# A long-convolution block with a dense block behind it: PSUM handed out by banks instead of bank pairs

## The chip, the cores and the metric

One core of one Trainium2 chip. The metric is the device time of one execution in microseconds; the time of a kernel is the median of its runs. Times inside a run come from one profiled execution of the same program.

## What is computed

The input is `A_q` (2048 positions of 640 channels), called x. The first block is a long convolution: `k` goes through a short causal filter of four taps per channel, is multiplied by `v`, then convolved along the whole sequence with a filter `ssm_k` per channel, and gates the normalized x. The second block is a dense layer with Mish and a dense layer back. Both add to their input.

```python
kv = k_shift * v                                   # k_shift: 4 taps per channel
y  = irfft(rfft(pad(kv)) * rfft(pad(ssm_k)))[:S] + kv * ssm_D
h  = x + layernorm(x) * y                          # S=2048, D=640
a  = layernorm(h) @ w1 + b1                        # F=1728
h2 = h + (a * tanh(softplus(a))) @ w2
```

## The kernel before, in words

The Fourier transforms are matmuls in two steps. Channels are five blocks of 128 (`NDC`), grouped in three chunks: blocks 0 and 1, blocks 2 and 3, block 4. The names that the steps use, in the order of the data:

- `k1` (L526 to L539): a block of `ssm_k` (`rn`, loaded by `d_n`, L439) is transposed on TensorE in 16 pieces and copied to `kk_s`; `dadd` (L541) adds `ssm_D` to the filter's first tap.
- `kt`, `kts`, `ks`, `kv` (L482 to L521): `k` is transposed, shifted by one on GpSimd, filtered by matmuls with the band matrices `wsh` (made from `coef` on GpSimd), and multiplied by `v` on VectorE out of PSUM.
- `s1k`, `s1v` (L446 to L470): the first step of the transform, for the filter and for kv, 16 matmuls of 64 rows a unit, 20 units each. `s2k` (22 units, L566) and `s2v` (20 units, L602) are the second step, with the table G (`d_g`).
- `sw`: DMAs that swap real and imaginary rows of the filter's transform; `p1`, `p2` (L617, L621): the product of the transforms on VectorE.
- `i1` (20 units, L653 and L654) and `i2` (one unit a position tile, three parts a, b, c, L713): the inverse. `y` copies an i2 unit out of PSUM.
- `ln1` (statistics of x on VectorE), `ln1p` (GpSimd), `lnx` (normalized x); `wb` and `h` (gate and sum), `bn` (statistics of h), `pow` (GpSimd), `hc` (normalized h), then a transpose to `lnhT` by TensorE (`trpe`, `trev`, first four tiles) or by DMA (`trd`, L750).
- `m1` (L789) and `hb` (Mish on ScalarE, L797): the dense layer in, by five units of 256, 256, 512, 512, 512 positions, 14 feature blocks each; `m2` (L807), `res` (addition, L814) and `d_out` (L816): the dense layer back, by 16 tiles of 128 positions.

Each of these is an operation with a name, an engine, what it depends on and the PSUM space that it takes. The order of the work is a list written out by hand, `ORDER` (L26): every word is an operation and its engine (t TensorE, a ScalarE, v VectorE, p GpSimd, d SyncE's DMA queue, s ScalarE's DMA queue). `_schedule` (L140) walks the list with a cost for each operation, gives each its planned start and its PSUM slot, and the operations are emitted in the order of planned starts. The engines then run their own instructions in that order and wait for each other by semaphores.

PSUM is four tiles, `ps0` to `ps3`, of two banks each (128 partitions by 1024 float32). A unit (`_RT(R_PS)`) takes one whole tile, TensorE fills both banks, and one instruction on ScalarE or VectorE empties both (`ev`, L365 to L369). The next unit that gets the tile waits for that. Even a small unit takes a whole tile.

The first DMAs stand in SyncE's queue: the constants `cst` (identity, the transform's cosines and sines, masks), then the filter blocks 1, 2, 0, 4, and so on; the shift taps and `ssm_D` stand in ScalarE's. Ten matmuls on zeros (`wm`, L389) run while the first loads are under way. The table for Mish is loaded by the instruction `warm` (L380).

Of the kernel before, what the change touches and what calls it, by code (L numbers as in the profile page):

```python
# [16 lines left out]
S = 2048  # L17
# [9 lines left out]
d_id:d d_n1:d cz:v d_n2:d wz:v wm:t cfpe:t coef:v k1pe1:t k1pe2:t k1ev2:v warm:a d_n0:d k1ev1:a k1pe0:t k1ev0:v d_n4:d k1pe4:t k1ev4:v kz:p wsh1:p  # L27
dadd1:p dadd2:p s1kpe2_0:t s1kpe2_1:t s1kpe2_2:t s1kev2_1:v d_a12:d d_k2:d dadd4:p s1kpe2_3:t s1kev2_0:a s1kev2_2:a s1kpe4_2:t d_k0:d s1kpe1_1:t
s1kev2_3:a d_n3:d s1kev4_2:v s1kpe4_0:t s1kpe1_0:t d_k1:d d_x0:d s1kev1_1:a dadd0:p wsh3:p s1kpe4_3:t s1kpe0_3:t s1kev4_0:v s1kev1_0:a d_k3:d
s1kev0_3:a s1kev4_3:v s1kpe4_1:t s1kev4_1:a k1pe3:t k1ev3:v ln1_2:v s1kpe0_1:t s1kpe0_2:t s1kev0_1:a s1kpe1_3:t ktpe1_0:t ktpe0_0:t ln1_1:v s1kev0_2:a  # L30
ktpe1_1:t s1kev1_3:a ktpe0_1:t ktpe1_2:t ktpe0_2:t ktpe2_0:t ktpe1_3:t d_v1:d ktpe0_3:t d_g6:d d_v0:d ktev1:v ktpe2_1:t ktpe3_0:t ktev0:a dadd3:p
ktpe2_2:t ktpe3_1:t ktpe2_3:t ktpe4_0:t ktev2:a ktpe3_2:t ln1_3:v ktsh0:p wsh0:p ktpe4_1:t ktpe3_3:t d_g7:d d_g3:d d_g2:d ktpe4_2:t ktpe4_3:t
s1kpe3_3:t ktev3:v s1kpe1_2:t s1kev3_3:a s1kpe0_0:t s1kpe3_0:t s1kev1_2:a ktev4:v ktsh4:p ktsh1:p s1kev0_0:v ln1_0:v s1kpe3_2:t s1kev3_0:a s1kpe3_1:t
kspe0_1:t s1kev3_1:a ln1p0:p kspe0_0:t s1kev3_2:a kspe4_0:t s2kpe_16:t s2kev_16:a kv0_1:v kv0_0:v kspe4_1:t kv4_0:v s2kpe_9:t s2kev_9:a kv4_1:v
kspe1_0:t s2kpe_6:t s2kev_6:a s2kpe_20:t kspe1_1:t d_g5:d d_g4:d d_g0:d ktsh2:p ln1p3:p wsh2:p kv1_0:v ktsh3:p s2kpe_18:t s2kev_20:a s2kpe_17:t
s2kev_18:a kv1_1:v s2kev_17:a kspe3_1:t s2kpe_8:t s2kev_8:a s2kpe_15:t kv3_1:v s1vpe0_3:t s2kev_15:a s1vpe1_0:t kspe3_0:t s2kpe_21:t s1vev0_3:v
s1vev1_0:a s2kpe_14:t kv3_0:v s2kev_21:a s2kpe_13:t s2kev_14:a s2kpe_19:t s2kpe_0:t s2kpe_11:t s2kev_13:v s2kev_19:a s2kev_0:a s2kpe_10:t s2kev_10:a
d_g1:d s2kpe_4:t s2kpe_12:t s2kev_11:v s2kev_4:v s2kev_12:a s1vpe1_1:t s1vev1_1:v s1vpe0_0:t s1vpe0_2:t s1vev0_2:v s1vpe0_1:t s1vpe1_3:t s1vev0_0:a
s1vev0_1:a s1vev1_3:a s1vpe1_2:t s1vev1_2:v s1vpe3_0:t s2kpe_1:t s1vev3_0:a s2kpe_2:t s2kpe_3:t s2kev_2:a s2kev_1:v kspe2_0:t s2kpe_7:t s2kev_3:v
s2kpe_5:t s2kev_7:a kv2_0:v sw0_1:d kspe2_1:t s2kev_5:a s2vpe0_4:t kv2_1:v s2vpe0_7:t s2vev0_4:a s2vpe0_1:t s2vev0_1:a s2vpe0_2:t s2vev0_2:a  # L40
s2vev0_7:v p2_0_4:v s1vpe4_3:t s2vpe0_3:t s2vev0_3:a s2vpe0_5:t s1vev4_3:v s2vpe0_6:t s2vev0_6:a s1vpe3_2:t s1vev3_2:a s2vev0_5:v p1_0_4:v p2_0_5:v
s1vpe2_1:t p2_0_6:v s1vev2_1:v p2_0_7:v s1vpe2_2:t s1vev2_2:a sw0_0:d s1vpe4_2:t s1vpe3_3:t s1vev4_2:a s1vev3_3:a s1vpe3_1:t s1vpe4_0:t s1vev4_0:v
s1vpe2_3:t p2_0_1:v p2_0_2:v s1vpe2_0:t s1vev3_1:a s1vev2_0:a s1vpe4_1:t s1vev2_3:a s2vpe0_0:t s2vpe1_7:t s2vev0_0:a s2vpe1_5:t s2vev1_7:a s2vev1_5:a
s2vpe1_2:t s2vpe1_0:t s2vev1_0:a s2vpe1_4:t s2vev1_4:a s1vev4_1:a p1_0_5:v p1_0_6:v p1_0_2:v p1_0_1:v sw1_0:d p2_0_0:v s2vev1_2:v p2_1_0:v p2_0_3:v
p1_0_0:v sw1_1:d p1_0_7:v p1_0_3:v p2_1_4:v s2vpe1_3:t s2vpe1_6:t s2vpe1_1:t d_x2:d sw2_1:d s2vev1_6:a s2vpe2_3:t s2vev1_3:a p2_1_3:v s2vev1_1:a
s2vev2_3:a s2vpe2_2:t p2_1_7:v p2_1_6:v p1_1_0:v i1pe0_1:t i1ev0_1:a p2_1_5:v p2_1_1:v s2vpe2_1:t s2vev2_1:a s2vev2_2:a sw2_0:d p2_1_2:v p1_1_4:v
p1_1_2:v p1_1_1:v p1_1_3:v p1_1_6:v p1_1_7:v i1pe0_2:t i1pe0_0:t i1ev0_0:a i1pe0_7:t i1ev0_7:a s2vpe2_0:t i1ev0_2:a i1pe0_4:t i1ev0_4:a s2vev2_0:a
i1pe0_6:t i1ev0_6:a i1pe0_3:t p1_1_5:v i1ev0_3:a i1pe0_5:t i1ev0_5:a i1pe1_2:t i1pe1_0:t i1pe1_6:t i1ev1_0:a i1ev1_6:a i1pe1_1:t i1ev1_1:a i1pe1_7:t
p2_2_2:v p1_2_2:v p2_2_3:v d_w11:d d_w13:d i1ev1_2:a i1ev1_7:a p2_2_1:v p2_2_0:v p1_2_1:v p1_2_0:v i1pe1_4:t i1ev1_4:a p1_2_3:v ln1_15:v ln1_11:v
ln1_12:v i1pe2_2:t i1pe1_3:t i1ev2_2:v i1ev1_3:a i1pe2_0:t i1pe2_1:t i1ev2_1:v i1ev2_0:a i1pe1_5:t ln1_13:v d_w14:d d_t2m:d d_w12:d i1pe2_3:t d_x1:d  # L50
i1ev1_5:a d_w10:d d_w2:d i2pa0:t i2pa1:t i2pb0:t i2pa2:t i2pb1:t i1ev2_3:a i2pc0:t y0:a i2pc1:t d_small:p y1:v b1pe:t i2pb2:t ln1p2:p i2pc2:t w1z:p
ln1p1:p gate:p lnx0:p c_b1:a y2:a lnx1:p i2pa9:t i2pa3:t i2pb9:t i2pc9:t y9:a i2pb3:t i2pa12:t i2pc3:t y3:a i2pb12:t i2pa7:t i2pc12:t y12:a i2pb7:t
i2pa4:t i2pc7:t y7:a lnx3:p ln1p15:p lnx2:p wb1:v wb0:v i2pb4:t i2pa13:t h0:v h1:v bn0:v ln1p13:p pow0:p i2pc4:t y4:a bn1:v i2pb13:t i2pa5:t i2pc13:t
y13:a i2pb5:t i2pa14:t i2pc5:t hc0:v i2pb14:t trpe0:t pow1:p y5:a wb2:v hc1:v i2pc14:t y14:a i2pa10:t trpe1:t i2pb10:t trev0:v i2pa15:t wb3:v i2pa11:t
i2pb15:t i2pb11:t i2pc15:t i2pc10:t trev1:a i2pc11:t m1pe0_6:t y10:a y15:a m1pe0_0:t hb0_0:a y11:a m1pe0_2:t m1pe0_5:t hb0_6:a hb0_2:a hb0_5:a i2pa6:t
m1pe0_4:t ln1_7:v ln1p7:p h3:v ln1p12:p h2:v bn3:v pow3:p bn2:v lnx7:p ln1_4:v pow2:p hc2:v hc3:v i2pb6:t trpe2:t i2pc6:t m1pe0_3:t ln1_6:v lnx12:p
ln1p11:p lnx11:p ln1p6:p hb0_4:a ln1_8:v ln1_9:v ln1_5:v ln1_14:v trpe3:t y6:a trev2:a trev3:a w2z:p ln1p4:p lnx4:p m1pe0_1:t m1pe1_0:t hb0_3:a
m1pe1_1:t hb0_1:a lnx6:a wb4:v hb1_1:a ln1p9:p ln1p8:p ln1p5:p m1pe1_6:t lnx15:a wb6:v i2pa8:t hb1_6:a m1pe1_2:t i2pb8:t m1pe1_4:t i2pc8:t hb1_2:a
h4:v bn4:v pow4:p hb1_0:a lnx13:a lnx5:p ln1_10:v ln1p10:p wb5:v wb15:v wb13:v h13:v hc4:v wb7:v m2pe1:t m1pe1_3:t lnx10:a y8:v h5:v bn5:v hb1_3:a
pow5:p h7:v h6:v bn7:v pow7:p hc5:v bn6:v lnx8:a res1:v wb8:v lnx9:a hb1_4:a trd4:d pow6:p trd5:d wb10:v h10:v hc6:v trd6:d m1pe1_5:t hb1_5:a m2pe0:t  # L60
hc7:v res0:v m2pe2:t m2pe3:t h8:v bn8:v res2:v trd7:d m1pe2_3:t pow8:p wb12:v m1pe2_2:t wb11:v h11:v h15:v hc8:v res3:v bn10:v wb9:v bn15:v h9:v
m1pe2_0:t hb2_0:a hb2_2:a pow10:p d_out3:d m1pe2_6:t hc10:v bn11:v pow11:p bn9:v trd8:d hc11:v ln1p14:p pow9:p hc9:v h12:v m1pe2_4:t m1pe2_1:t hb2_3:a
hb2_6:a m1pe2_5:t lnx14:a hb2_1:a hb2_5:a bn12:v trd11:d pow12:p hb2_4:a bn13:v trd10:d trd9:d m1pe3_2:t pow15:p wb14:v h14:v bn14:v pow14:p hc12:v
trd12:d m1pe3_0:t hc15:v d_out2:d m1pe3_5:t hb3_5:a hb3_2:a hb3_0:a m1pe3_4:t m2pe6:t m1pe3_6:t hc14:v trd15:d trd14:d d_out0:d hb3_4:a hb3_6:a
m1pe3_1:t m1pe3_3:t res6:v pow13:p hb3_1:a hb3_3:a hc13:v m2pe5:t m2pe4:t m2pe7:t trd13:d d_out6:d res5:v res4:v d_out4:d res7:v m2pe11:t m2pe10:t
res11:v res10:v m1pe4_6:t m1pe4_0:t hb4_0:a hb4_6:a m2pe8:t m1pe4_2:t m1pe4_1:t hb4_2:a m1pe4_4:t m1pe4_5:t hb4_4:a m1pe4_3:t hb4_1:a m2pe9:t hb4_3:a
res9:v hb4_5:a res8:v m2pe14:t m2pe15:t res14:v m2pe13:t d_out7:d d_out9:d d_out5:d d_out11:d d_out1:d res13:v res15:v d_out13:d d_out14:d m2pe12:t
res12:v d_out15:d d_out10:d d_out8:d d_out12:d
""".split()
UNITS = [256, 256, 512, 512, 512]  # L70
# [13 lines left out]
class _Ring:  # L84
# [3 lines left out]
    def free(self):  # L88
        best = None
        for i, rt in enumerate(self.held):  # L90
            t = 0.0
            for u in rt.users if rt is not None else ():
                if not u.done:
                    break
                t = max(t, u.finish + u.lat + _TAIL[u.eng] + _HOP)
            else:
                if best is None or t < best[0]:
                    best = (t, i)
        return best


class _RT:


    def __init__(self, ring):
        self.ring = ring
        self.users = []
        self.tile = None


class _Op:
    def __init__(self, name, opts, deps, allocs, uses, emit, prio, lat):
        self.name = name
        self.opts = opts
        self.deps = [d for d in deps if d is not None]
# [24 lines left out]
def _schedule(ops):  # L140
# [6 lines left out]
    for word in ORDER:  # L147
# [24 lines left out]
        for rt in o.allocs:  # L172
            rt.slot = rt.ring.free()[1]
            rt.ring.held[rt.slot] = rt
# [9 lines left out]
def _dve1(n):  # L184
    return 0.06 + 0.001045 * n
# [671 lines left out]
```

## Time and profile before

| | us |
|---|---|
| runs: median (lowest to highest) | 231.36 (230.88 to 232.72) |
| profiled execution, its own time | 229.75 |
| its span, first to last instruction | 227.9 |
| TensorE busy | 217.6 (95%) |
| VectorE busy | 143.4 (63%) |
| ScalarE busy | 132.5 (58%) |
| GpSimd busy | 51.6 (23%) |

How to read it: the span is cut into stretches, and busy time in a stretch says which engine is full there. A share over the whole span is an average over stretches with different limits. Matmuls overlap in the array, so that a TensorE that is busy is not yet at its peak; the distance between the starts of two matmuls is their price. The same holds for casts on ScalarE and VectorE: one lasts longer than the distance to the next. The chain of waits leads back from the last instruction to what released it, step by step.

### The profile page before, as it was taken

The numbers are of one execution on the slowest core, as the hardware profiler recorded it, in microseconds if no ns is written. First come the engines' busy times: TensorE is split into PE (matmuls) and PEld (weight loads), VectorE is DVE, ScalarE is ACT, GpSimd is POOL, SyncE is SP. The second block draws the span as 40 slices with busy tenths as digits, with TensorE's granted clock in tenths as the row PEclk, the third lists the DMA queues.
The fourth block names the chain that finished last, engine by engine and source line by source line (L and its number), as shares of the span: only waits on it lengthen the run. The fifth ranks groups of instructions, "written<-read, shape, count | busy, mean of one in ns | idle before, by whom it ended". The sixth has DMA issues, their size and how long they took to land.

```text
span 227.9 us, 6283 instructions
## 1 busy us (share of the span) xinstructions
PE 217.6 (95%) x2718; PEld 164.6 (72%) x2718; DVE 143.4 (63%) x289; ACT 132.5 (58%) x180; POOL 51.6 (23%) x87
## 2 busy tenths in 40 slices
PE   7989999999879999989999999999999999999993
PEld 2889899999768999878877754445567766447772
DVE  0697998999999999899999998810202120002121
ACT  2388979989999999878966004748240004244000
POOL 0550675000000546149852113210000000000000
PEclk9999999999999999999999999999999999999999
DMA  6999991066898495930001421442200100000304
GB/s 189 417 396 423 415 405 39 4 186 171 250 265 237 109 344 183 384 126 1 3 0 29 83 64 20 69 91 58 58 0 3 58 0 3 0 0 1 117 4 169
DMA packets 27086, 30.60 MB, mean 134 GB/s; under 512 B 9201, under 2 KB 23474, under 8 KB 26674
## 3 DMA queue, kind: packets, MB, share of 16 engines
q1 hardware_dynamic: 26944, 30.19, 40.7%
q8 instruction: 21, 0.34, 0.7%
q14 instruction: 7, 0.06, 0.1%
q10 hardware_dynamic: 50, 0.01, 0.0%
q0 software_dynamic: 64, 0.00, 0.0%
HBM read 20.37 MB, written 2.62 MB: 101 GB/s over the span
## 4 chain that ended last, share of the span: by engine, by line
PE 79%; ACT 9%; DVE 5%; DMA 3%; issue 2%; SPq 1%; POOL 0%; DVEq 0%; ACTq 0%
PE ps L807 27%; PE ps L789 27%; ACT uv L367 7%; PE ps L654 4%; PE ps L653 4%; PE ps L460 4%; DMA rn<-in_A_ssm_k_dram 3%; PE ps L566 2%; PE ps L490 2%; ACT uk L367 2%; PE ps L713 2%; PE ps L513 2%; PE ps L461 2%; DVE uv L369 2%; PE ps L602 2%
## 5 line engine op out<-in xcount | busy, mean ns | idle before, releaser
L797 ACT ACTIVATE uv<-ps,b1s 128x512 bf16<-128x512 f32 (+1 forms) x70 | 36.5, 608 | 59.8 <-PE ps L789 59.8
L789 PE MATMUL ps<-G 128*128 128x512 bf16 (+1 forms) x350 | 62.5, 336 | 0.0
L807 PE MATMUL ps<-rn,uv 128*128 128x320 bf16 x448 | 61.8, 299 | 0.0
L807 PEld LDWEIGHTS <-uv 128*128 128x128 bf16 x448 | 43.8, 98 | 17.5
L789 PEld LDWEIGHTS <-G 128*128 128x128 bf16 x350 | 34.1, 98 | 25.8
L367 ACT CAST uk<-ps 128x1024 bf16<-128x1024 f32 (+2 forms) x50 | 46.6, 1093 | 6.3 <-PE ps L461 3.8
L814 DVE TENSOR_TENSOR xa<-ps,xa 128x640 bf16<-128x640 f32 x6 | 4.9, 823 | 49.0 <-PE ps L807 49.0
L367 ACT CAST uv<-ps 128x1024 bf16<-128x1024 f32 x30 | 28.5, 1095 | 0.0
L653 PE MATMUL ps<-a,uv 128*128 128x128 bf16 x160 | 18.7, 219 | 0.0
L653 PEld LDWEIGHTS <-uv 128*128 128x128 bf16 x160 | 17.8, 113 | 0.1
L738 POOL TENSOR_TENSOR r<-ve,mhalf 128x1 f32<-128x1 f32 x16 | 9.5, 595 | 28.5 <-DVE ve L735 28.4
L814 DVE TENSOR_TENSOR xb<-ps,xb 128x640 bf16<-128x640 f32 x6 | 4.9, 823 | 17.1 <-PE ps L807 14.9
L692 POOL TENSOR_TENSOR r<-ve,mhalf 128x1 f32<-128x1 f32 x16 | 12.7, 797 | 6.9 <-DVE ve L688 6.8
L602 PE MATMUL ps<-uv,G 128*128 128x64 bf16 (+1 forms) x384 | 12.6, 187 | 1.7 <-ACT uv L367 1.7
L369 DVE CAST uk<-ps 128x1024 bf16<-128x1024 f32 (+1 forms) x12 | 13.9, 1191 | 0.4 <-ACT uk L367 0.2
L602 PEld LDWEIGHTS <-G 128*128 128x128 bf16 x384 | 11.7, 96 | 2.4 <-issue 2.2
L617 DVE TENSOR_TENSOR uv<-uv,uk 128x1024 bf16<-128x1024 bf16 x20 | 12.6, 688 | 0.1
L519 DVE TENSOR_TENSOR ra<-ps,rb 128x1024 bf16<-128x1024 f32 x10 | 11.7, 1218 | 1.0 <-PE ps L514 1.0
L369 DVE CAST uv<-ps 128x1024 bf16<-128x1024 f32 x10 | 12.0, 1220 | 0.3 <-PE ps L461 0.2
L460 PE MATMUL ps<-cst,ra 128*64 128x128 bf16 x160 | 10.8, 219 | 1.1 <-ACT uv L367 0.8
L461 PE MATMUL ps<-cst,ra 128*64 128x128 bf16 x160 | 11.0, 221 | 0.0
L713 PE MATMUL ps<-uk,ra 128*128 128x256 bf16 (+1 forms) x96 | 10.7, 255 | 0.2
(103 smaller groups left out, 337.3 us busy)
## 6 DMA issues: line engine op xcount, KB each, us to landing
G<-tab_g SPq DMA_DIRECT2D x8, 512.0 KB, 13.5
rn<-in_A_ssm_k_dram SPq DMA_DIRECT2D x5, 512.0 KB, 5.6
ra<-in_A_k_dram SPq DMA_DIRECT2D x4, 640.0 KB, 7.6
rb<-in_A_v_dram SPq DMA_DIRECT2D x2, 1280.0 KB, 11.0
G<-in_B_w_dram SPq DMA_DIRECT2D x5, 432.0 KB, 6.1
rn<-in_B_w_dram SPq DMA_DIRECT2D x1, 2080.0 KB, 11.5
rn<-uk SPq DMA_DIRECT2D x4, 512.0 KB, 6.5
rb<-uk SPq DMA_DIRECT2D x8, 256.0 KB, 7.7
```

Of the source, the lines that this page charges most:

```text
L367: nc.scalar.copy(o, i)
L369: nc.vector.tensor_copy(o, i)
L460: nc.tensor.matmul(ps[0:64, dgl, :], lhs, mc, start=True, stop=True)
L461: nc.tensor.matmul(ps[64:128, dgl, :], lhs, ms, start=True, stop=True)
L602: nc.tensor.matmul(ps[:, fl * st:fl * st + n], g_v[:, f0 + fl, :], V[c.i][:, :, f0 + fl, :], start=True, stop=True)
L617: nc.vector.tensor_tensor(v, v, K[c.i][:, :, f0:f1, :], ALU.mult)
L653: nc.tensor.matmul(pz[:, dgl, :], V[c.i][:, dg // 4, :, dg % 4], a12[:, 0, :], start=True, stop=False)
L692: nc.gpsimd.tensor_tensor(r1[:, t2:t2 + 1], ve1[:, t2:t2 + 1], mhalf[:, 0:1], ALU.pow)
L713: nc.tensor.matmul(py[:, o:o + w], t2m[:, t2, ri, :], Z[c.i][:, ri * NT + t2, o - c.c0:o - c.c0 + w], start=(ri == 0), stop=(ri == 1))
L789: nc.tensor.matmul(ph[:, i * 512:i * 512 + w], w1[:, dc, fc * P:fc * P + P], lnhT_of(u)[:, dc, 0:w], start=(dc == 0), stop=(dc == NDC - 1))
L797: nc.scalar.activation(hb_of(u)[:, fc, 0:w], rt.tile[:, i * 512:i * 512 + w], ACT.Mish, bias=b1s[:, fc:fc + 1], scale=1.0)
L807: nc.tensor.matmul(po[:, a * 512:a * 512 + 320], hb_of(u)[:, fc, tl * P:(tl + 1) * P], w2[:, fc, a * 320:a * 320 + 320], start=(fc == 0), ...
```

## The change

- PSUM is given out by single banks. The four tiles stay, and a slot is now one half of a tile (eight slots); a unit can still take both halves of a tile. Of two banks that are free equally early the one is taken whose neighbour comes free later.
- The units of `k1`, `ks`/`kv`, `s1k`, `s1v`, `s2k`, `s2v` and `i1` can be done in halves, x and y: half of the matmuls into one bank and an eviction of that bank. The list chooses for each: nearly all `s1`, `s2k`, `ks`, `i1` units are halves, 10 of 20 `s2v` units are whole. `m1` is 70 units of one feature block instead of 35 of two; `m2` and `res` are two halves of 320 columns a tile, 448 and 192 for the last tile, whose output DMA is also in two parts.
- The filter block 1 is loaded and transposed by halves of 64 partitions (`d_n1a`, `d_n1b`), and block 0 is loaded first.
- The identity is a table of its own; identity, the rest of the constants, the shift taps and `ssm_D` are four DMAs in ScalarE's queue. `wm` has seven matmuls instead of ten.
- `ORDER` is a new list throughout. Among other things it has `warm` behind four copies and a cast on ScalarE, the first half of V behind seven blocks of G, the last piece of x behind `w2`, and five `ln1` instead of eight ahead of the last `i1` eviction.

The core of the diff:

```diff
+class _Banks(_Ring):
+    def free(self, est, wide):
+        t = [self.when(i) for i in range(len(self.held))]
+        if wide:
+            i = min(range(0, len(t), 2), key=lambda i: max(t[i], t[i + 1]))
+            at = max(t[i], t[i + 1])
+        else:
+            i = min(range(len(t)), key=lambda i: (max(t[i], est), -t[i ^ 1]))
+            at = t[i]
+        assert at < 1e9
+        return at, i
...
-    R_PS = _Ring(4)
+    R_PS = _Banks(8)
...
     def ps_f32(rt):
-        rt.tile = banks[rt.slot][:]
+        o = rt.slot % 2 * 512
+        rt.tile = banks[rt.slot // 2][:, o:o + (1024 if rt.wide else 512)]
         return rt.tile
...
+        if not whole_only and (_BOTH or ev_name + "x" in names):
+            for h in range(2):
+                rt = _RT(R_PS, False)
+                pes.append(OP(pe_name + "xy"[h], ("pe", dur / 2), deps, allocs=[rt], emit=lambda e, rt=rt, h=h: pe(ps_f32(rt), h)))
+                outs.append(OP(ev_name + "xy"[h], evs(cols // 2), pes[-1:], uses=[rt], emit=lambda e, rt=rt, h=h: evf(e, rt.tile, h)))
...
-        for _ in range(10):
+        for _ in range(7):
             nc.tensor.matmul(ps[:, 0:512], wz[:, 0:P], wz[:, P:D], start=True, stop=True)
...
+    d_id = OP("d_id", ("dmaS", 0.42), emit=lambda e: nc.scalar.dma_start(idn[:], dram["idn"]), lat=1.4)
+    d_cst = OP("d_cst", ("dmaS", 0.42), emit=lambda e: nc.scalar.dma_start(cst[:], dram["cst"]), lat=3.3)
...
+    def emit_kn1(h):
+        return lambda: nc.sync.dma_start(raw_n[1][64 * h:64 * h + 64], A_ssm_k.rearrange("(d m l) s -> m d l s", m=NDC, l=4)[1, 16 * h:16 * h + 16])
...
-        for fp in range(NFC // 2):
-            rt = _RT(R_PS)
+        for fc in range(NFC):
+            rt = _RT(R_PS, False)
...
+            for a, (d0, d1) in enumerate(((0, 448), (448, D)) if t2 == NT - 1 else ((0, 320), (320, D))):
+                rt = _RT(R_PS, False)
...
+                    DMA(f"d_out{t2}{'ab'[a]}", 164e3 * (d1 - d0) / D, (lambda t2=t2, d0=d0, d1=d1: nc.sync.dma_start(oview[:, t2, d0:d1], xt(t2)[:, d0:d1])), deps=outs[-1:])
```

## The prediction

> **What bounds the kernel now.** I read the page's slices first, then busy time by stretch, then the chain, then the timelines of ScalarE and VectorE for prices.
>
> ```profile
> PE   7989999999879999989999999999999999999993
> DVE  0697998999999999899999998810202120002121
> ACT  2388979989999999878966004748240004244000
> ```
>
> Forty slices of 5.7 us. TensorE looks full everywhere; VectorE is full up to slice 23 and ScalarE up to slice 16, then both have room. Stretch by stretch:
>
> ```profile
> 5.90:11.60 5.70, 5.40 (x87) 4.93 (x88) 3.94 (x7) 1.87 (x1) 2.94 (x3) 1.00 1.03 417
> 11.60:30.00 18.40, 17.15 (x423) 16.09 (x418) 15.90 (x27) 16.74 (x17) 7.25 (x9) 1.00 1.02 411
> 30.00:40.00 10.00, 10.00 (x192) 9.60 (x189) 9.31 (x8) 8.50 (x11) 6.86 (x12) 1.00 0.49 192
> 40.00:70.80 30.80, 27.97 (x725) 25.75 (x722) 30.31 (x38) 30.15 (x35) 0.00 (x0) 1.00 0.67 187
> 70.80:91.10 20.30, 20.27 (x388) 19.76 (x386) 19.99 (x45) 20.01 (x22) 9.66 (x10) 1.00 0.65 206
> 91.10:101.10 10.00, 9.19 (x98) 7.64 (x96) 8.84 (x27) 8.24 (x15) 2.04 (x4) 1.00 0.81 292
> 101.10:133.30 32.20, 32.20 (x275) 26.09 (x274) 30.72 (x89) 19.20 (x40) 17.42 (x31) 1.00 0.11 22
> 133.30:224.30 91.00, 90.95 (x546) 53.26 (x544) 23.11 (x54) 26.27 (x43) 4.99 (x9) 1.00 0.16 41
> ```
>
> Columns: PE, PEld, DVE, ACT, POOL busy, PE clock, DMA share, GB/s. From 40 to 91 us VectorE and ScalarE, which empty PSUM, are over 98% busy: the front is bound by evictions. From 101 us on TensorE is never idle:
>
> ```profile
> 101.06 4.42 PE ps L789 x40
> 121.87 11.41 PE ps L807 x84
> 133.28 23.74 PE ps L789 x110
> 205.23 19.03 PE ps L807 x140
> 224.28 0.82 DVE xb L814
> ```
>
> L789 runs at 0.216 us for 512 columns, L807 at 0.136 for 320, back to back. So the end is the moment the first L789 can start (101.06), plus 123.2 us of matmuls, plus the tail. The change can win only ahead of 101 us and in the tail.
>
> ```profile
> 7.13 1.87 ACT L367 COPY xa<-ps 128x2048 bf16<-128x2048 bf16 x1 [3.92 <-PE ps L534]
> 11.65 4.68 ACT L367 CAST uk<-ps 128x1024 bf16<-128x1024 f32 x5 [2.65 <-PE ps L461]
> 52.31 20.26 ACT L367 CAST uv<-ps 128x1024 bf16<-128x1024 f32 x22
> 94.28 4.27 ACT L367 CAST rb<-ps 128x640 bf16<-128x640 f32 x7 [0.35 <-PE ps L713]
> ```
>
> ```profile
> 13.63 3.49 DVE L369 CAST uk<-ps 128x1024 bf16<-128x1024 f32 x3 [0.20 <-ACT uk L367]
> 119.32 0.82 DVE L369 CAST rb<-ps 128x640 bf16<-128x640 f32 x1
> 120.06 0.48 DVE L728 TENSOR_TENSOR xa<-rb,xa 128x640 bf16<-128x640 bf16 x1
> ```
>
> Here is the price of a half. One cast lasts 1.10 us (group mean), so 22 in 20.26 us are (20.26-1.10)/21 = 0.91 apart; at 640 columns (4.27-0.69)/6 = 0.60. The slope is 0.82 ns a column, the fixed part 0.07. VectorE: (3.49-1.22)/2 = 1.135 apart at 1024, 0.74 at 640 (119.32 to 120.06): fixed part 0.08.
>
> **The front, as one account of two engines.** The last i1 eviction ends near 92.2 on ScalarE, and VectorE's share of that stage near 91.1. ScalarE first evicts at 7.13, VectorE at 8.37: together 85.1 + 82.7 = 167.8 us, of which the stretches (without the early coef work, and with ScalarE's last microsecond) give 156.7 busy. Idle: 11.1 us over both. Now the terms, counted in the two lists of operations up to the same point.
>
> Halves: ScalarE gets 127 half evictions for 63.5 whole ones, VectorE 73 (20 of them the kv products, 6 bf16 ones) for 36.5. 63.5 x 0.07 + 36.5 x 0.08 = 7.3 us. Bounds: nothing, and 15.6 with fixed parts of 0.157 (Mish rows: 0.577 apart at 512, 0.367 at 256) and 0.155 (VectorE's durations, 1.22 and 0.82). I take the cast rows, which are the same instruction.
>
> Second table load: ScalarE's list now starts with a copy, whose table is loaded ahead of it, and `warm` comes inside the stream: 1.28 + 0.20 us (its rows at 1.71 and 3.01, idle time before). +1.5.
>
> Layer statistics: five ln1 groups instead of eight ahead of that point, 3 x 1.23 = -3.7. Units moved between the engines (five 1024-column ones to VectorE, some s2k and k1 ones to ScalarE), and coef, whose 1.0 us now falls into the stream: +2.7.
>
> Earlier start. The first filter block is SP's first DMA (0.73 for 1.15) and took 4.7 us to its first matmul, so 5.4; eight transposes of 0.067 and a hop: ScalarE at 6.1, not 7.13. VectorE takes the half block behind it at 7.0, not 8.37. -2.4. The three warming matmuls taken out (0.43 each) only end TensorE's cover at 4.4 instead of 5.8. The constants on ScalarE's queue cost four issues of about 0.5 us before 2.6, covered by the empty wait; identity, second there, lands about 2.3 us after 1.15. In SP's queue the first half of V now stands behind seven table blocks: 12.2 MB at 0.41 MB/us from 2 us on, and a landing, about 33 us. VectorE has 28.9 us of listed work ahead of its use, so 36: covered by 3 us. Later there the last piece of x stands behind w2 (2.16 MB, 5.3 us more, landing near 99); its statistics come after hc1, near 103: covered by 4 us. On POOL's queue the w2 zeroing (0.63) and two ln1p (1.16 each) stand ahead of lnx0, 5.6 us in all after the gate, which is due some 8 us before the last i1 eviction: covered.
>
> Sum: 7.3 + 1.5 - 3.7 + 2.7 - 2.4 = +5.4 us over two engines, 2.7 us for the front, plus half of whatever the idle time changes. That last term decides. Zero idle would give 2.7 - 5.6 = -2.9; break-even needs 5.7 of the 11.1 us to go.
>
> Does handing out single banks remove idle time? The tiles ps0 to ps3 still have two banks each, and the changed program's waits are by tile: 86 of the 222 waits that a matmul has for an eviction are for the eviction of its tile's other bank, and 81 of the 166 waits that evictions have for TensorE are for matmuls into the other bank (before: 33 and 20, all at the two-bank m1 units or behind them). So a half is often released only with its neighbour, as a whole unit was; and where plan and program differ, the in-order queues behind stall too. Against that, the other half of the waits is really finer. At the head the profile's 2.65 us gap on ScalarE shrinks to about 1.1 (copies end near 8, first cast near 9), but VectorE gets a new one of about 2.3: its second piece stands behind s1 matmuls that wait for POOL's dadd (0.45). I take idle as before, 11.1.
>
> **Behind the front.** Up to the first m1 unit, 9.9 us today, the change does 12.6 instead of 14 i2 tiles; VectorE's own list (four half evictions 2.4, one ln1 1.2, wb to hc 5.4, transpose and copy about 1.2) is 10.2, so TensorE idles longer: +0.7 (0 to +1.5). The m1 and m2 matmuls keep count and columns; their waits by tile are covered by ScalarE's 65 and VectorE's 68 idle us of 91 (0 to +1). Tail: the last addition has 192 columns, 0.35 for 0.82, and a third of the bytes: -0.6.
>
> Total 2.7 + 0.7 - 0.6 = +2.8: 229.75 becomes 232.55 in the profiled execution. The runs' median, 231.36, lies 1.6 above that execution, so 234.2.
>
> [...] Row: 0.07 and 0.08 us per extra instruction. [...] Row: one table load 1.28 us. [...]
>
> **The rivals.** A: finer hand-out works. Idle falls to the head's 1.1 us, -5.0: 229.2; with the halves' fixed part at its lower bound, nothing, 3.65 less, 225.5; the middle is 227.4. For it: the other waits are for the own bank, and two engines can take one unit's halves at once. Against: the waits by tile. It decides once idle is under 5.7.
> B: idle is halved, -2.8: 231.4, no change. For it: only half of the waits are by tile.
> C: stalls pile up. 54 evictions ahead of m1 wait for a neighbour's fill, 0.22 to 0.45 us each; at 0.22 that is 12 us more idle, +6: 240.2. Against: in a full queue the neighbour is filled long before.
> D: the fixed part is the larger one of the rows, +4.1: 238.3. For it: Mish at 256. Against: the cast rows.
>
> **Chances.** Forecast, idle about as before, 0.32; C and D together 0.14; B 0.36; A 0.18. One per cent is about what a measurement of this kernel can tell from no change. Faster (under 229.0) is A: 0.18. Within it is B: 0.36. Slower (over 233.7): forecast, C and D, 0.46. The range, 227.4 to 238.6, runs from A's middle to D and leaves out half of A and half of C and D; the forecast's own is 232.6 to 236 (idle 8 to 15).
>
> **What would show it.** Right: 512-column casts 0.49 apart on ScalarE and 0.61 on VectorE; first evictions near 6.1 and 7.0; ScalarE and VectorE together still idle 9 to 13 us up to the last i1 eviction, at 94 to 96; first m1 near 104; a table load inside the first casts. Wrong: the last i1 eviction before 92, or halves under 0.46 apart, or matmuls of m1 and m2 no longer back to back.

## The result, and the profile after

The changed kernel takes 265.66 us (265.23 to 266.19), beside 231.12 (229.76 to 232.72) of the kernel before on the same chip: a ratio of 1.149, interval 1.1415 to 1.1571. The sign is that of the forecast, the size is not: +34.5 us where +2.8 was expected, far outside the range.

The 40 slices of the profile's page, for TensorE, VectorE, ScalarE and TensorE's clock:

```profile
PE   6797888777677898898799999899989898979892
DVE  0187887777799899498869996761640000100422
ACT  1568896886899898777477515450011666110000
PEclk9689999999999999999999999999999999999999
```

Before, VectorE stood at 9 in all slices but one from 40 to 136 us, and ScalarE at 8 or 9 up to 91 us. Now, in the slices from 13 to 73 us, VectorE stands at 7 or 8 and ScalarE mostly at 6 or 8, and the front has become longer. The busy time by stretch says it in numbers (columns as before: stretch, its length, then PE, PEld, DVE, ACT, POOL busy, clock, DMA share, GB/s):

```profile
40.00:70.80 30.80, 23.75 (x471) 21.11 (x468) 22.55 (x39) 23.97 (x46) 0.84 (x2) 1.00 0.37 111
70.80:91.10 20.30, 15.31 (x428) 13.56 (x425) 18.75 (x35) 17.95 (x27) 0.00 (x0) 1.00 0.73 220
...
123.90:260.20 136.30, 126.09 (x821) 79.80 (x827) 57.99 (x167) 46.30 (x82) 24.14 (x44) 1.00 0.12 31
```

From 40 to 71 us all three engines are busy for about 75% of the time: no engine is full there, and what fills the rest is waiting. And the dense layers, 123.2 us back to back before, take 136.35, 10.2 of which TensorE idles. Here are pieces of the chain of waits from their end (start, length, engine; L888 is Mish, L899 m2, L904 its addition):

```profile
233.65 0.69 ACT uv L888
...
247.32 0.51 DVE xb L904
247.87 2.08 PE ps L899 x14
249.96 0.50 DVE xb L904
250.51 7.78 PE ps L899 x56
258.31 0.50 DVE xb L904
258.86 1.33 PE ps L899 x14
260.21 0.49 DVE xa L904
```

Before, the chain ran through matmuls alone here. Now it runs through single Mishes and additions too, and behind each of those shown but the last TensorE had stopped for it.

The whole difference splits into three stages. The last column is the experiment that decides most of it, told below: the changed program on tiles of one bank.

| us | before | after | after, one-bank tiles |
|---|---|---|---|
| first eviction, ScalarE / VectorE | 7.13 / 8.37 | 6.71 / 9.84 | 6.56 / 8.55 |
| busy up to the last i1 eviction, both engines | 156.9 | 170.2 | 165.2 |
| idle up to there, both engines | 11.0 | 43.5 | 8.0 |
| last i1 eviction (mean of the two engines) | 91.7 | 115.1 | 94.1 |
| first m1 | 101.06 | 123.86 | 102.16 |
| from there to the end of the last m2 matmul | 123.2 | 136.35 | 124.07 |
| from there to the end of the span | 3.66 | 4.20 | 3.03 |
| span | 227.9 | 264.4 | 229.3 |

### The profile page after: what moved, and what is told of

Read it like the earlier page. It is cut to its first block, busy times and chain, and to the rows that moved or that the text cites. A ratio compares the mean times of both kernels' runs of the same rounds, so it can differ in the third digit from the quotient of the medians.

```text
span 264.4 us, 6418 instructions
## 1 busy us (share of the span) xinstructions
PE 226.7 (86%) x2724; PEld 168.5 (64%) x2731; DVE 149.5 (57%) x343; ACT 142.5 (54%) x245; POOL 48.2 (18%) x88
## 4 chain that ended last, share of the span: by engine, by line
PE 59%; ACT 18%; DVE 8%; DMA 5%; issue 4%; SPq 3%; POOLq 0%; ACTq 0%; POOL 0%; DVEq 0%
PE ps L899 22%; PE ps L883 21%; ACT uk L421 9%; ACT uv L421 6%; PE ps L809 3%; ACT uv L888 3%; DVE uk L423 2%; DMA rn<-in_A_ssm_k_dram 2%; DVE ra L590 2%; SPq L679 2%; PE ps L749 2%; DMA G<-in_B_w_dram 2%; PE ps L662 2%; PE ps L635 2%; PE ps L750 1%
## 5 line engine op out<-in xcount | busy, mean ns | idle before, releaser
L888 ACT ACTIVATE uv<-ps,b1s 128x512 bf16<-128x512 f32 (+1 forms) x70 | 38.2, 604 | 53.8 <-PE ps L883 45.3
L899 PE MATMUL ps<-rn,uv 128*128 128x320 bf16 (+2 forms) x448 | 63.4, 299 | 4.1 <-DVE xb L904 1.7
L899 PEld LDWEIGHTS <-uv 128*128 128x128 bf16 x448 | 43.6, 98 | 23.2 <-issue 4.5
L421 ACT CAST uk<-ps 128x512 bf16<-128x512 f32 (+2 forms) x95 | 50.1, 593 | 13.4 <-PE ps L750 2.4
L421 ACT CAST uv<-ps 128x512 bf16<-128x512 f32 (+1 forms) x46 | 29.9, 720 | 5.0 <-PE ps L699 1.8
L904 DVE TENSOR_TENSOR xa<-ps,xa 128x320 bf16<-128x320 f32 x12 | 5.6, 485 | 41.8 <-PE ps L899 41.8
L423 DVE CAST uk<-ps 128x512 bf16<-128x512 f32 (+2 forms) x27 | 17.5, 673 | 7.9 <-ACT uk L421 5.8
L904 DVE TENSOR_TENSOR xb<-ps,xb 128x320 bf16<-128x320 f32 (+2 forms) x12 | 5.5, 487 | 25.1 <-PE ps L899 25.1
L834 POOL TENSOR_TENSOR r<-ve,mhalf 128x1 f32<-128x1 f32 x16 | 10.3, 645 | 41.3 <-DVE ve L831 41.3
L423 DVE CAST uv<-ps 128x512 bf16<-128x512 f32 x21 | 14.0, 688 | 4.3 <-PE ps L536 2.5
L662 PE MATMUL ps<-uk,G 128*128 128x160 bf16 x128 | 13.1, 230 | 3.7 <-ACT uk L421 2.0
L535 PE MATMUL ps<-cst,ra 128*64 128x128 bf16 x160 | 11.8, 219 | 4.8 <-ACT uv L421 3.1
L590 DVE TENSOR_TENSOR ra<-ps,rb 128x512 bf16<-128x512 f32 x20 | 13.0, 687 | 5.0 <-ACT uk L421 3.8
L421 ACT CAST rb<-ps 128x640 bf16<-128x640 f32 x16 | 10.5, 695 | 8.6 <-PE ps L809 8.6
L715 DVE TENSOR_TENSOR uv<-uv,uk 128x1024 bf16<-128x1024 bf16 x20 | 13.1, 687 | 0.0
```

The lines of the kernel that those rows point to most:

```text
L421: nc.scalar.copy(o, i)
L423: nc.vector.tensor_copy(o, i)
L535: nc.tensor.matmul(ps[0:64, k, :], lhs, mc, start=True, stop=True)
L590: nc.vector.tensor_tensor(kv_w[:, m, :, 8 * h:8 * h + 8, l0:l0 + n], ps.rearrange("p (l t d) -> p d t l", l=n, t=8), raw_v[:, 8 * h:8 * h ...
L662: nc.tensor.matmul(ps[:, o:o + 160], g_v[:, f, :], KA[:, :, f, :], start=True, stop=True)
L715: nc.vector.tensor_tensor(v, v, K[c.i][:, :, f0:f1, :], ALU.mult)
```

## The experiments

Theory 1: the plan gives banks away one by one, but the tiles of PSUM still have two banks and the program waits by tile, so a bank also waits for what happens in its neighbour. The rivals: the price of the additional instructions (2), the head with its clock, table load and DMA queue (3), the new order itself (4).

**Tiles of one bank.** Order, plan and slots stay.

```diff
-    banks = [psum.tile([P, 1024], F32, name=f"ps{i}") for i in range(4)]
+    banks = [psum.tile([P, 512], F32, name=f"ps{i}") for i in range(8)]
...
+        rt.tile = banks[rt.slot][:]
+        if rt.wide:
+            rt.tile = [rt.tile, banks[rt.slot + 1][:]]
...
-            outs.append(OP(ev_name, evs(cols), pes[-1:], uses=[rt], emit=lambda e, rt=rt: evf(e, rt.tile, None)))
+            outs.append(OP(ev_name, evs(cols), pes[-1:], uses=[rt], emit=lambda e, rt=rt: evf(e, rt.tile[0], None) if whole_only else [evf(e, rt.tile[h], h) for h in range(2)]))
...
```

> The changed kernel with PSUM as eight tiles of one bank instead of four of two; same order, same slots; the 35 or so units that take two banks are emptied by two instructions. Theory 1 (the plan gives out banks, but the program waits by tile, so that every half also waits for its neighbour's matmuls and evictions, in the front and in the dense layers): most of the 34 us go, 226 to 238 us, first m1 at 95 to 105, m1 and m2 back to back again (first m1 to last m2 123 to 125). Theory 2 (the fixed price of the halves): two instructions more for each wide unit, 266 to 269. Theory 3 (the head: half clock, second table load, x0 in front of the table G in SP's queue): within 3 us of 265.7. Theory 4 (the new order itself is worse, whatever the waits): over 250.

Measured: 231.39 us, ratio to before 1.0037 (1.0016 to 1.0058). All of the loss but about 1 us is gone, from all three stages. Order, plan and head are those of the changed kernel, so theory 4 (over 250 us) is out, and theories 2 and 3 cannot be the bulk of the loss: the halves and the head are all still there. By stretch:

```profile
40.00:70.80 30.80, 28.72 (x725) 26.16 (x723) 30.21 (x51) 30.80 (x66) 0.00 (x0) 1.00 0.72 205
70.80:91.10 20.30, 20.11 (x400) 19.53 (x398) 19.53 (x40) 19.84 (x42) 2.56 (x6) 1.00 0.69 239
...
102.10:226.20 124.10, 123.72 (x822) 79.96 (x828) 57.87 (x168) 46.44 (x88) 23.96 (x44) 1.00 0.14 35
```

ScalarE is busy for all 30.80 us of the first stretch, where it had 23.97. Its timeline between 40 and 62 us, first of the changed kernel, then of this one:

```profile
42.00 3.03 ACT L421 CAST uk<-ps 128x480 bf16<-128x480 f32 x6 [0.43 <-DVE ra L590]
46.17 1.49 ACT L421 CAST uk<-ps 128x480 bf16<-128x480 f32 x3 [1.15 <-DVE ra L590]
48.06 1.95 ACT L421 CAST uk<-ps 128x480 bf16<-128x480 f32 x4 [0.41 <-PE ps L662]
50.37 0.56 ACT L421 CAST uk<-ps 128x480 bf16<-128x480 f32 x1 [0.36 <-DVE ra L590]
```

```profile
39.67 8.90 ACT L422 CAST uk<-ps 128x480 bf16<-128x480 f32 x19
48.33 1.23 ACT L422 CAST uv<-ps 128x512 bf16<-128x512 f32 x2
49.28 0.74 ACT L422 CAST uk<-ps 128x480 bf16<-128x480 f32 x1
49.73 13.03 ACT L422 CAST uv<-ps 128x512 bf16<-128x512 f32 x26
```

The releaser in the brackets is the tell. A ScalarE cast of the filter (uk) needs nothing that VectorE's kv product (ra, L590) makes; they meet only in a tile of PSUM. On tiles of one bank these brackets are gone. The changed kernel's list of waits has more of the kind, evictions held by the other engine's evictions:

```profile
DVE uk L423 <- ACT uk L421: 5.8, 5, 3.4
DVE ra L590 <- ACT uk L421: 3.8, 6, 1.1
```

The columns are microseconds in all, times, and the longest. With the smaller lines of its kind in the front that is 22 waits and 15.5 us over the two engines. The kernel before has two (1.7 us), the program on tiles of one bank none.

**The dense layers alone.** The kernel before, its front and order unchanged, with slots of one bank on tiles of two, single banks for m1, m2 and the small units, and the last tile in two parts.

```diff
-    R_PS = _Ring(4)
+    R_PS = _Banks(8)
...
-        for fp in range(NFC // 2):
-            rt = _RT(R_PS)
+        for fc in range(NFC):
+            rt = _RT(R_PS, False)
```

> The kernel before with one part of the change: slots of one bank on tiles of two, one bank for the small units, m1 in 70 units of one bank, m2 and its addition in halves, the last tile in two parts; the front's units and the order stay. Theory 1: the front stays as before (first m1 near 101), but m1 and m2 are no longer back to back: first m1 to last m2 128 to 137 instead of 123.2, and the run 236 to 246. Theories 2, 3, 4 (the cause lies in the front alone): 229 to 232; the tail alone would give 0.6.

Measured: 250.17, ratio 1.0864 (1.0813 to 1.0915). First m1 at 102.1, the stage 142.3 instead of 123.2. Theory 1 holds, and the loss is over its upper end. TensorE's and ScalarE's timeline where the third group of positions starts m1:

```profile
135.56 6.64 PE L813 MATMUL ps<-G 128*128 128x512 bf16 x29
...
142.24 0.69 ACT L818 ACTIVATE uv<-ps,b1s 128x512 bf16<-128x512 f32 x1 [15.06 <-PE ps L813]
142.98 1.24 PE L813 MATMUL ps<-G 128*128 128x512 bf16 x5 [0.78 <-ACT uv L818]
...
144.25 2.42 ACT L818 ACTIVATE uv<-ps,b1s 128x512 bf16<-128x512 f32 x4 [1.33 <-PE ps L813]
144.99 1.24 PE L813 MATMUL ps<-G 128*128 128x512 bf16 x5 [0.78 <-ACT uv L818]
```

Six units of five matmuls fill banks (29 of the 30 matmuls are in the trace). The first Mish in ScalarE's list empties the fifth (its tile's first half), but it starts only when the sixth, in the other half, is done. The next matmuls wait 0.78 us for this Mish; the next Mish waits 1.33 us for these, and the matmuls behind them 0.78 us for it. TensorE and ScalarE take turns, twice here and again at 153, 162 and 172 us.

**The same units, on tiles of one bank.** Every two-bank eviction of the front is then two instructions.

> The kernel before with its own order and whole units, on eight tiles of one bank: every eviction of two banks in two instructions, each bank released by itself; m1 in 70 units, m2 in halves, the last tile in two parts as in the change. Theory 1 (waits by tile): m1 and m2 back to back (first m1 to last m2 123 to 124), where the same units on tiles of two banks took 142; the front has the fixed price of the halves (first m1 at 105.4 with whole release) less what the finer release gives: first m1 at 102 to 105, run 231 to 234.5. If small units as such break the dense layers: 245 or more.

Measured: 232.30, ratio 1.0072 (1.005 to 1.0093); first m1 at 104.40, the stage 123.4. At the same place of the program:

```profile
136.62 9.66 PE L824 MATMUL ps<-G 128*128 128x512 bf16 x44
...
142.22 0.69 ACT L829 ACTIVATE uv<-ps,b1s 128x512 bf16<-128x512 f32 x1 [14.35 <-PE ps L824]
143.30 3.00 ACT L829 ACTIVATE uv<-ps,b1s 128x512 bf16<-128x512 f32 x5 [0.39 <-PE ps L824]
```

The first Mish starts 5.60 us after the first matmul (five units of 1.09), where it took 6.68 (six units), and TensorE does not stop. Small units as such cost the dense layers next to nothing.

**Mish earlier in the program.** On tiles of two banks again, each Mish right behind its own m1 unit in the order in which the program is written down.

```diff
+    for o in [o for o in order if o.name.startswith("hb")]:
+        order.remove(o)
+        order.insert([p.name for p in order].index("m1pe" + o.name[2:]) + 1, o)
```

> The kernel before with single banks in the dense layers on tiles of two (250.2), with one edit: each Mish stands in the program right behind the m1 unit that it empties, instead of where its planned start puts it. Theory 1 (waits by tile): the Mish no longer waits for the matmuls of the next unit in its tile's other bank, but these now wait for the Mish, about 0.9 us for most of the 35 pairs: first m1 to last m2 150 to 165, the run 256 to 272. Rival (the evictions only stand too late in the program, and a bank waits for its own eviction alone): matmuls back to back, 229 to 234.

Measured: 272.51, ratio 1.1818 (1.1783 to 1.1853), the stage 164.9 us; the run is half a microsecond over the upper end. The rival is out by 38 us. The waits of the dense layers:

```profile
PEld L813 <- issue: 37.3, 37, 1.6
PE ps L813 <- ACT uv L818: 26.1, 34, 1.1
```

The second line is 34 waits of the m1 matmuls for a Mish, nearly one for each of the 35 pairs of units, where the late Mish had nine (6.9 us); the first line is the idle time of TensorE's weight loads ahead of m1. This order turns the false wait round and does not take it away.

**The price of halves alone.** The kernel before, its two-bank evictions ahead of m1 as two instructions each, for example:

```diff
-                ev(e, (V, K)[which][c.i][:, b0:b0 + 2, :, :], ps)
+                for h in range(2):
+                    ev(e, (V, K)[which][c.i][:, b0 + h:b0 + h + 1, :, :], rt.tile[:, 512 * h:512 * h + 512].rearrange("p (b g f) -> p b f g", b=1, g=4))
```

> The kernel before with each of its two-bank evictions ahead of m1 (k1, s1, kv, s2k, s2v, i1) as two instructions of one bank each; units, order and tiles stay. This is the fixed price of halves alone. The recorded price, 0.07 us on ScalarE and 0.08 on VectorE for each further instruction, some 8 us over two engines that share the work: 3 to 5 us, 234 to 236. Theory 2 (the fixed price is what costs 34 us): over 245. Theory 1 is not touched: 233 to 236.

Measured: 234.11, ratio 1.0157 (1.0124 to 1.0189); first m1 at 105.4. The page's first line:

```profile
PE 218.8 (94%) x2712; PEld 165.2 (71%) x2718; DVE 146.0 (63%) x325; ACT 137.4 (59%) x260; POOL 51.5 (22%) x87
```

ScalarE is busy for 4.9 us more than before with 80 more instructions, VectorE for 2.6 with 36 more: 0.06 and 0.07 us each, close to the recorded price. Theory 2 explains some 3.6 us of the 34.5 (with 116 more instructions, where 100 were counted for the change).

**The head.** In the changed kernel, on its tiles of two banks: ten warming matmuls again, `warm` ahead of ScalarE's first copy, x0 issued behind the last piece of k and three blocks of G. `move(a, b)` takes the operation a out of the program's order and puts it ahead of b.

```diff
-        for _ in range(7):
+        for _ in range(10):
...
+    move("warm", "d_n1a")
+    move("d_x0", "ln1_3")
+    move("d_g1", "d_x0")
+    move("d_g0", "d_x0")
```

> The changed kernel with its head mended: ten warming matmuls instead of seven, Mish's table loaded ahead of the first copy, the first piece of x issued behind k's last piece and three blocks of G instead of ahead of them. Theory 3: TensorE's clock stays full up to 15 us, the DMA queues are not starved at 18 to 23 us, and at least 10 us go: 255 or less. Theory 1: the head gets 1 to 3 us shorter and the rest stays: 262 to 265, first m1 at 120 to 123. Theory 2 and 4: as theory 1, 262 to 266.

Measured: 265.55, ratio 1.1527 (1.1482 to 1.1573), first m1 at 124.7: nothing. Theory 3 falls for the table load, x0 and the number of warming matmuls; even the 1 to 3 us that theory 1 gave to the head are not there. The DMA queues were no longer starved (416 and 367 GB/s from 11 to 20 and from 20 to 30 us, where the changed kernel had 364 and 235), but that made nothing faster. The half clock was not removed (0.56 instead of 0.51 between 8.5 and 15.4 us, see the last section), so its own price stays open. It is not the bulk: on tiles of one bank the early transposes ran slowly too (16 in 1.86 us), and the run took 231.4.

The same three edits on tiles of one bank:

> The changed kernel on eight tiles of one bank (231.4) with its head mended as before: ten warming matmuls, Mish's table loaded ahead of the first copy, x0 issued behind k's last piece and three blocks of G. If the head costs anything once the waits are by bank: ScalarE has 1.3 to 1.5 us less in a front where it is full, half of it counts, and the loads come sooner: 230.0 to 230.9. If the head is hidden anyway: 231.0 to 231.8.

Measured: 234.97, ratio 1.0168 (1.0133 to 1.0203): 3.6 us worse than without them, which neither line expected. Two of them were then tried alone.

> The changed kernel on eight tiles of one bank (231.4, ratio 1.0037) with one of the three head edits alone: Mish's table loaded ahead of the first copy. The recorded price of the second table load is 1.28 + 0.20 us of ScalarE in a stream where ScalarE is full from 20 us on; half of it counts: 230.5 to 231.0. If the load falls into time in which ScalarE would wait anyway: 231.2 to 231.8. The slower time with all three edits (235.0) is put down to x0 alone, on which VectorE waited 2.4 us; if it were the table load, this run would be over 233.

Measured: 231.53, ratio 1.0033 (1.0016 to 1.005): the second table load is hidden on these tiles.

> The changed kernel on eight tiles of one bank (231.4) with another of the three head edits alone: x0 issued behind k's last piece and three blocks of G instead of ahead of them. The three together took 235.0, the table load alone 231.5. If x0's late landing is the cause (VectorE waited 2.4 us for it, with the evictions of k behind it): 233.5 to 235.5. If it is the ten warming matmuls and the clock: 231 to 232.

Measured: 233.74, ratio 1.0138 (1.0105 to 1.017): x0 is most of it. VectorE's waits between 15 and 45 us:

```profile
DVE st L784 <- DMA x<-in_A_q_dram: 1.5, 1, 1.5
```

The statistics of x (L784) stand in VectorE's list ahead of the evictions of k, so x0 behind three blocks of G holds them all. The order of the change was right there. The remaining 0.3% lie within the intervals of the two runs, and the ten warming matmuls were not tried alone.

**The tail.** The kernel before with the last m2 unit as 448 and 192 columns in two whole tiles.

```diff
+            if t2 == 12:
+                for a, (d0, d1) in enumerate(((0, 448), (448, D))):
+                    rt = _RT(R_PS)
...
-res12:v d_out15:d d_out10:d d_out8:d d_out12:d
+res12a:v res12b:v d_out15:d d_out10:d d_out8:d d_out12a:d d_out12b:d
```

> The kernel before, on its tiles of two banks, with the part of the change that needs no single banks: the last m2 unit as 448 and 192 columns in two tiles, each with its own addition and output DMA. The tail gets 0.5 to 0.7 us shorter, all else stays: ratio 0.997 to 0.998, 229.6 to 229.8 beside 230.3. If the extra output DMA at the end costs as much as the shorter addition gives: 1.000.

Measured: 230.00, ratio 0.9959 (0.9935 to 0.9983). This is the only version here that is faster than the kernel before, by 0.4%.

## Why the prediction was wrong, step by step

- *The front is bound by evictions, the dense layers by matmuls back to back*: right for the kernel before, and again for the changed one on tiles of one bank.
- *Halves, +7.3 us over two engines*: right, +7.5 in the experiment. The larger price that was weighed, rival D's fixed parts of 0.157 and 0.155 us (15.6 for the change), is out for these casts: 116 more instructions cost 7.5 us, and by those parts they would have cost 18.1 (80 x 0.157 + 36 x 0.155). But in the changed kernel the busy time grew by 13.3, over the 7.8 that all the terms of work gave (8.3 on tiles of one bank, with 19 more instructions): a cast that follows another lies 0.50 us behind it (13.03 us for 26), and one that stands alone takes its whole 0.58. Casts that were pulled apart by waits took more busy time here for the same work.
- *Second table load, +1.5*: it is in the trace, at 12.78 us, and on tiles of one bank it costs nothing (231.39 with it, 231.53 with it moved ahead). ScalarE has gaps there in any case: with the load moved away, it idles 3.3 us ahead of 14.8 in that run. ScalarE's own time for it is the 1.28 and 0.20 us put in, with gaps of 0.02 and 0.01 us around the load: in the changed kernel the cast ahead ends at 12.76, the load runs from 12.78 to 14.06, and the next instruction, `warm` itself, starts at 14.07.
- *Earlier start, -2.4*: failed, +1.05 in the changed kernel, -0.4 on tiles of one bank. ScalarE starts at 6.7 and 6.6, not 6.1, and VectorE at 9.84 and 8.55, not 7.0. On tiles of one bank the 16 transposes of block 0 run from 5.52 to 7.38, 1.86 us where 0.067 each had been put in (1.07), and those of the half block only then. On tiles of two banks these 16 took 1.16 us, but each engine's first copy waited for the matmuls into its tile's other bank as well: ScalarE's, at 6.71, for all 16 (from 5.52), VectorE's, at 9.84, for those of the other half block (8.60 to 9.81).
- *"I take idle as before, 11.1"*: this is the first step that decides. It was 43.5. Rival C had the mechanism, 54 evictions that wait for a neighbour's fill, and mis-sized it (12 us), as it priced each wait by one fill, and once. It also counted waits of evictions for matmuls alone: the 22 waits of evictions for the other engine's evictions, 15.5 us, are in no term. And the lines of the dense layers show a loop instead of a single wait: the eviction is late by a fill, so the matmul behind it is late by an eviction, and the next eviction by that. Each such wait also holds all that stands behind it in two in-order lists. How the 43.5 us divide over these was not measured; on tiles of one bank they are gone together, and idle is 8.0. The argument against C, that in a full queue the neighbour is filled long before, did not hold in the dense layers: of the six units ahead of the first Mish above, its neighbour was the last to be filled.
- *"their waits by tile are covered by ScalarE's 65 and VectorE's 68 idle us of 91 (0 to +1)"*: the second step that decides. It cost 13.1 us here, and 19.1 with the order of before. Idle time of ScalarE covers nothing when ScalarE idles because it waits for TensorE. The lines on the turns show it: ScalarE has 1.33 us free ahead of the second Mish, and TensorE still waits 0.78 for it.
- *Up to the first m1, +0.7*: failed, it fell from 9.4 to 8.75 (from the mean of the two engines' last i1 evictions).
- *The transfers*: right for V's first half and x's last piece; after the first filter blocks no wait for a DMA stands in the changed kernel's list of waits. For the identity it was not: it lands 4.3 us after its issue at 1.15, not 2.3, and the first transpose, at 5.52, waits 1.1 us for it. That this start lies near the 5.4 put in for the filter block is luck.
- *Tail, -0.6*: right where the banks are free of each other (-0.6, and -0.8 alone). On the changed kernel's tiles it is +0.5: the last addition but one starts at 260.21, when the last matmuls in its tile's other bank are done, and three output DMAs are then issued one behind the other.
- *Rival B, idle halved, 231.4*: this comes nearest to what the change does once the program waits as the plan thinks. But idle fell by a quarter, from 11.0 to 8.0, and not by half, and that the run took 231.4 is luck: the kernel before took 230.28 beside it. Rival A's point of decision, 5.7 us of idle gone, is not reached even then.

The count was on record, 86 of 222 waits by tile, and so was most of the mechanism. What failed was to price it by what one wait lasts, to leave out that the two engines' evictions hold each other, and to cover the rest with averages. A plan that itself counts the neighbour's users was not tried, so how much of the loss a better order could save on tiles of two banks stays open.

## What to carry to other kernels

A plan is worth what the program can carry out: the unit in which a resource is handed out must be the unit in which the program waits for it. When a count of waits shows that the two differ, follow one such wait round through both in-order queues until it closes on itself; if it closes, price it by its period, and let no idle time cover it. Finer hand-out of PSUM gained only a quarter of the front's idle time here (11.0 to 8.0 us over two engines), and the instructions that it adds cost more (7.5 us).

## What the runs showed of the hardware that was not expected

TensorE's clock record has a half-speed stretch at 8.5 us in the changed kernel; its third column from the end below is the clock. With ten warming matmuls instead of seven the same stretch reads 0.56 (on tiles of two banks).

```profile
8.50:15.40 6.90, 6.02 (x72) 5.85 (x73) 2.60 (x5) 3.13 (x5) 1.53 (x4) 0.51 1.03 414
```

So three warming matmuls more do not keep the clock up here. In the run on tiles of one bank the column reads 1.00 from 4.5 to 15.4 us, though the 16 transposes of block 0 took 1.86 us there, where the changed kernel's took 1.16 us: at the very start the spacing is the better witness. What the slow stretch costs is open: in the line above TensorE is busy for 6.02 of 6.90 us, and ScalarE and VectorE for 3.13 and 2.60, so here the evictions do not set the pace; no run removed it.
